# An input tile without padding, a mean transformed once, and a second tile for a rounded angle, in an adaLN kernel with an S4D convolution and a token mixer

## The chip, the cores and the metric

The kernel runs on one core of one Trainium2 chip. The metric is the device time of one execution in microseconds (us), and lower is better. One core has TensorE (PE, matmuls; its weight loads are listed as PEld), VectorE (DVE), ScalarE (ACT), GpSimd (POOL) and SyncE (SP), which issues most of the DMA transfers. Each engine works through its own instructions in order; engines wait for each other by semaphores. SBUF is the on-chip memory of 128 partitions, PSUM the memory that matmuls write.

## What is computed

The input `A_u` has 2048 tokens of 448 channels. The reference, cut to what matters:

```python
mod = (silu(c) @ w_mod)                     # six vectors: sa, ca, ga, sb, cb, gb
h = layernorm(x) * (1 + ca) + sa
x = x + ga * A_ref(h)                       # S4D: a long convolution per channel
h = layernorm(x) * (1 + cb) + sb
x = x + gb * B_ref(h)                       # mixer: an MLP over the tokens

def A_ref(u):
    A = -exp(log_A_real) + 1j * A_imag;  C = (C_real + 1j * C_imag) * dt
    P = exp((A * dt)[:, :, None] * arange(L))        # 448 x 256 x 2048
    K = 2 * einsum("dn,dnl->dl", C, P).real
    y = irfft(rfft(u^T, 2L) * rfft(K, 2L))[:L]
    return y^T + u * D_skip
```

## The kernel before

**The convolution kernel K.** The 448 channels are cut into 28 groups of 16, each in two halves of the 256 states, so 56 steps `s`, and these into seven windows of eight. Per channel and state a complex exponential is needed. Its exponents and phases come from matmuls against a table (`tab`) with rows `lex` and `lph`; ScalarE turns them into magnitudes (`mag`) and sines and cosines (`xe`, `xg`, `gs`); GpSimd multiplies the `G` factors (lines 716 and 717) and `m` (line 696), VectorE the `E` factors (lines 718 to 722); TensorE contracts them in `st_kgen` (line 743). At the start of a window `window(s)` makes the magnitudes of its eight steps.

**Parameters.** The rows in `lex` and `lph` are prepared for 128 channels at a time, q = 0 to 3. `chain(q)` is a generator whose small steps on VectorE are taken a few at a time, by `more(n)`, between other work. Its `split` writes a value as a high and a low part (`hl`, two buffers) on GpSimd and stores both to DRAM (`pars`, line 406), from where the groups load them. `phase()` leaves the parts of a phase in `ph` and `p64`, with `u` as a scratch tile; `angles()` follows and rounds an angle. For q of 2 and 3 `angles()` comes right after `phase()`, for q = 1 they stand apart.

**The transform of the input.** `x_load` puts the input rows into `xt`, [128, 16, 450]: a partition holds 16 successive tokens of 448 channels, each row followed by two spare columns. Twenty DMAs do this, each for 32 partitions and two or four rows; twelve are issued by SyncE, eight by GpSimd. `u_stats` (lines 543, 544) makes mean and variance of each token on VectorE. At step 8 `u_scale` makes the inverse deviations `rs` and writes the negative mean of each token into the first spare column, and `u_table` scales the transform's table `wu` by `rs`. `u_rows` then runs 32 times: a matmul of a scaled table with one row of `xt` and its mean column, 449 columns, and on VectorE an eviction (line 574) that adds the mean's column to the others and multiplies by `mod[1]`. Two evictions fill a tile `yt` (three buffers), which SyncE stores to `yu_d`. `u_cols` (lines 606, 610) is the second half of the transform, from step 17 on, evicted as `uo`. Later `xt` also receives parts of `w_mod`.

**Order.** PE, ACT, DVE and POOL run in the order in which the program issues their instructions. SyncE's DMAs run in written order up to step 8; from there to the last part of the convolution a planner orders them. The lists `act` and `dve` hold evictions that `flush` issues later on that engine. In the window at step 8 the first pass of the loop (`e == 0`) ends with seven warm-up matmuls, `warm(7)`, on TensorE; from the second pass on each has rows of `u_rows`. PSUM tiles of the transforms share three buffers (`pms`, tag `ms`).

After the 56 steps come the products in frequency, the inverse transform, the second layernorm, and the mixer (lines 1377 to 1379 and 1540 to 1542), which takes the second half of the time.

Of the kernel before, what the change touches and what calls it, by code (L numbers as in the profile page):

```python
# [11 lines left out]
F32 = mybir.dt.float32  # L12
# [3 lines left out]
ALU = mybir.AluOpType  # L16
# [5 lines left out]
L, D, N, F = 2048, 448, 256, 1792  # L22
P = 128
# [10 lines left out]
MAGIC = 1.5 * 2.0**23  # L34
# [198 lines left out]
def tile_adaln_s4d_mixer(ctx, tc, i, out):  # L233
    nc = tc.nc
    x = i["A_u"][0]
# [9 lines left out]
    mod = [None] * 3 + [cp.tile([P, D], F32, name=f"mod{k}") for k in range(3, 6)]  # L245
# [7 lines left out]
    with ExitStack() as es:  # L253
        V, S, G, T = nc.vector, nc.scalar, nc.gpsimd, nc.tensor
        tt, ts, stt = V.tensor_tensor, V.tensor_scalar, V.scalar_tensor_tensor
# [11 lines left out]
        pms = es.enter_context(tc.tile_pool(name="pms", bufs=3, space=PSUM))  # L267
# [8 lines left out]
        xp = spec.enter_context(tc.tile_pool(name="xp", bufs=1))  # L276
# [25 lines left out]
        nc.sync.dma_start(ldt[:, 1:3], ldt_v[P : 3 * P].rearrange("(q p) -> p q", p=P))  # L302
        for k in range(2):
            nc.sync.dma_start(ldt[64 * k : 64 * k + 64, 3:4], ldt_v[3 * P : D].rearrange("(q p) -> p q", q=1))
        xt = xp.tile([P, 16, D + 2], F32, name="xt")

        def x_load(r0, n, eng=nc.sync):
            for g in range(4):
                to = xt[32 * g : 32 * g + 32, r0 : r0 + n, 0:D]
                (nc.sync if r0 > 7 and g < 2 else eng).dma_start(to, x.rearrange("(s n h r) d -> h s n r d", s=2, h=2, r=16)[g // 2, g % 2, :, r0 : r0 + n])  # L310


        mg = cg.tile([P, 2, P], BF16, name="mg")
# [18 lines left out]
        wu = xp.tile([P, P], F32, name="wu")  # L332
# [12 lines left out]
        for q in range(4):  # L345
            r = slice(32 * q, 32 * q + 1)
# [32 lines left out]
        dve, act, aside = [], [], []  # L379
# [7 lines left out]
        def chain(q):  # L387


            n = min(P, D - P * q)  # L390
            f = N * n // P
            cr, ci, a, aim = (raws[q][nm][:, 0:f] for nm in ("A_C_real", "A_C_imag", "A_log_A_real", "A_A_imag"))
            xa, ya, s, t, u, ph, p64 = (
                qp.tile([P, N], F32, tag=nm, name=nm)[:, 0:f] for nm in ("xa", "ya", "s", "t", "u", "ph", "p64")
            )

            def split(src, places):
                hl = qp.tile([P, 2, N], F32R, tag="hl", name="hl", bufs=2)[:, :, 0:f]
                eng = G if aside or q == 1 else V
                eng.tensor_copy(hl[:, 0], src)  # L400
                yield
                eng.tensor_tensor(hl[:, 1], src, hl[:, 0].bitcast(F32), ALU.subtract)
                for k, v in places:
                    for m in range(P // n):
                        to = pars[q][v, k, 0:n, :, m * f : (m + 1) * f]
                        nc.sync.dma_start(to, hl[n * m : n * m + n].bitcast(F32))
                yield


            def phase():  # L410
                ts(ph, aim, dt4[:, q : q + 1], None, ALU.mult)
                yield
                ts(u, ph, MAGIC, MAGIC, ALU.add, ALU.subtract)
                yield
                tt(ph, ph, u, ALU.subtract)
                yield
                yield from split(ph, [(0, 0)])

                ts(u, ph, MAGIC7, MAGIC7, ALU.add, ALU.subtract)
                yield  # L420
                tt(p64, ph, u, ALU.subtract)
                yield
                yield from split(p64, [(1, 0)])

            def angles():
                ts(xa, xa, 4 * i2p, -0.5, ALU.mult, ALU.add)
                yield
                ts(cr, cr, 0.0, 0.5, ALU.is_ge, ALU.subtract)
                yield
                tt(xa, xa, cr, ALU.mult)  # L430
                yield
                ts(ci, ci, 0.0, 0.5, ALU.is_ge, ALU.subtract)
                yield
                stt(xa, xa, 0.5, ci, ALU.add, ALU.mult)
                yield
                stt(xa, ph, 63.0, xa, ALU.mult, ALU.add)
                yield
                ts(p64, xa, MAGIC, MAGIC, ALU.add, ALU.subtract)
                yield
                tt(xa, xa, p64, ALU.subtract)  # L440
                yield
                yield from split(xa, [(2, 0)])

            for to, src in (xa, cr), (ya, ci):
                if q > 1:
                    S.activation(to, src, AF.Abs, scale=0.5)
                else:
                    ts(to, src, -0.5, None, ALU.mult)
                    yield
                    stt(to, src, 0.5, to, ALU.mult, ALU.max)  # L450
                    yield
            tt(s, xa, ya, ALU.add)
            yield
            tt(ya, ya, xa, ALU.subtract)
            yield
            ts(s, s, 2.0**-120, None, ALU.max)
            yield
            V.reciprocal(xa, s)
            yield
            tt(ya, ya, xa, ALU.mult)  # L460
            yield

            ts(t, s, 2.0**-40, 2.0**80, ALU.is_lt, ALU.mult)
            yield
            stt(s, t, 1.0, s, ALU.max, ALU.mult)
            yield
            if q == 1:
                while not late_steps:
                    yield "logs"
                yield from phase()  # L470
            tmp[q] = a, s, u, xa, ya
            while q in tmp:
                yield "logs"
            if q == 1:
                yield from angles()
            ya = u
            yield from split(a, [(0, 1), (1, 1)])
            stt(s, t, -80 * math.log(2.0) / 2.0**80, s, ALU.mult, ALU.add)
            yield
            stt(s, ya, 0.5, s, ALU.mult, ALU.add)  # L480
            yield
            ts(s, s, ldt2[:, q : q + 1], None, ALU.add)
            yield
            yield from split(s, [(2, 1)])
            yield "exponents"

            if q > 1:
                yield from phase()

            if q > 1:  # L490
                yield from angles()
# [45 lines left out]
        mv = xp.tile([P, 16, 2], F32, name="mv")  # L537
        rs = xp.tile([P, 16], F32, name="rs")
        nm = xp.tile([P, 16], F32, name="nm")

        def u_stats(r):
            st = xp.tile([P, 6], F32, tag="st", name="st", bufs=2)
            V.bn_stats(st, xt[:, r, 0:D])
            V.bn_aggr(mv[:, r], st)

        def u_scale():

            tt(nm, rs, rs, ALU.mult)
            stt(nm, mv[:, :, 1], EPS, nm, ALU.add, ALU.mult)
            ts(nm, nm, -0.5, 1.5, ALU.mult, ALU.add)  # L550
            tt(rs, rs, nm, ALU.mult)
            ts(xt[:, :, D : D + 1], mv[:, :, 0:1], -1.0, None, ALU.mult)

        yts, wurs = {}, {}

# [5 lines left out]
        def u_rows(n):  # L561

            R, g = divmod(n, 4)
            gp, gl = divmod(g, 2)
            if gl == 0:
                yts[R, gp] = xp.tile([P, 2, D], F32, tag="yt", name="yt", bufs=3)
            if g == 0 and R < 6:
                u_table(R + 2)
            pm = pms.tile([P, D + 1], F32, tag="ms", name="pu")
            p = slice(64 * gl, 64 * gl + 64)  # L570
            T.matmul(pm, wurs[R][p, gp], xt[p, 2 * R + gp, 0 : D + 1], start=True, stop=True)

            def out():
                stt(yts[R, gp][:, gl], pm[:, 0:D], pm[:, D : D + 1], mod[1], ALU.add, ALU.mult)
                if gl:
                    nc.sync.dma_start(
                        yu_d[:, :, :, R, 2 * gp : 2 * gp + 2].rearrange("o k c g d -> (o k c) (g d)"),
                        yts.pop((R, gp)).rearrange("p g d -> p (g d)"),
                    )

            dve.append(out)
# [71 lines left out]
        def warm(n):  # L653

            g = made_k[0] // 2
            free = (kgs[g - 1] if g - 1 in kgs else kg_tile(g))[:, 4:8]
            for _ in range(n):
                T.matmul(free, ones[:, 0:P], ones[:, 0:256], start=made_k[0] % 2 == 0, stop=made_k[0] % 2 == 0, skip_group_check=True)
# [136 lines left out]
        pl, pu, pz, pv, pk = {}, {}, {}, {}, {}  # L795
# [232 lines left out]
        rows, cols, pieces = iter(range(32)), iter(range(16)), [0, 0]  # L1028
# [42 lines left out]
        def window(s):  # L1071
# [12 lines left out]
            for e in range(BATCH):  # L1084
# [30 lines left out]

                if s == 8 and e == 0:
                    warm(7)
                if s in (8, 16):
                    some(u_rows, rows, ((0, 2, 2, 2, 2, 0, 2, 2) if s == 8 else (2, 2, 2, 2, 2, 0, 1, 1))[e])
                elif s == 24 and e in (0, 2, 4, 6, 7):  # L1120
                    some(u_cols, cols, 1)
# [452 lines left out]
```

## Time and profile before

| | us |
|---|---|
| three runs | 669.04, 670.04, 670.37 |
| median | 670.04 |
| profiled execution | 668.55 |
| its span in the trace | 666.7 |
| PE busy | 615.8 (92%) |
| DVE busy | 442.9 (66%) |
| ACT busy | 440.4 (66%) |
| POOL busy | 269.7 (40%) |

The profile comes from one execution of its own. Times in its views are microseconds from the start of the span. A busy share is a mean over stages with different limits; POOL is idle in the second half. In a row of the timeline stand start, duration, engine, line, operation, output<-inputs and count, and in brackets the idle time before it and what ended that; rows of the same line next to each other are merged. "issue" stands for a wait that the profile cannot put down to anything. In a row of groups stand total busy time and mean nanoseconds of one.

### The profile page before, as it was taken

What the parts mean: (1) busy time and instruction counts of PE and PEld (TensorE: products, weight loads), DVE (VectorE), ACT (ScalarE), POOL (GpSimd) and SP (SyncE); (2) the same over time, 40 slices, a digit from 0 to 9 for tenths busy, and PEclk for the clock granted to TensorE, in tenths of its full rate; (3) what the DMA queues carried; (4) which work ended last, traced back from release to release, by engine and by line L of the source; (5) the groups of instructions that cost most, each with busy time, mean ns of one, the idle gap of its engine ahead of it and who ended that gap; (6) DMA issues with size and microseconds to landing.
All of it is one profiled execution on the core that took longest, in us unless ns stands there. A gap on an engine that the chain in (4) does not pass through costs nothing.

```text
span 666.7 us, 19151 instructions
## 1 busy us (share of the span) xinstructions
PE 615.8 (92%) x7637; PEld 445.0 (67%) x7637; DVE 442.9 (66%) x850; ACT 440.4 (66%) x828; POOL 269.7 (40%) x349
## 2 busy tenths in 40 slices
PE   1868899999899999999989899999999999999997
PEld 0545455445346565656645577788999999999997
DVE  8989789689696686869655678787522553333331
ACT  6978698899689999999678678886222532222220
POOL 7885588488589878797463000000000000000000
PEclk9998899999899899999999899999999999999999
DMA  6696747598775458567787999946664265555530
GB/s 157 191 215 174 253 157 247 197 257 260 221 236 175 107 128 215 168 185 222 210 281 238 262 243 249 220 125 200 169 189 137 71 188 161 165 162 167 163 116 28
DMA packets 99601, 125.14 MB, mean 188 GB/s; under 512 B 13780, under 2 KB 81144, under 8 KB 99512
## 3 DMA queue, kind: packets, MB, share of 16 engines
q1 hardware_dynamic: 98568, 121.30, 63.9%
q0 software_dynamic: 944, 2.62, 1.6%
q8 instruction: 60, 0.98, 0.6%
q14 instruction: 29, 0.24, 0.1%
HBM read 88.53 MB, written 34.87 MB: 185 GB/s over the span
## 4 chain that ended last, share of the span: by engine, by line
PE 60%; DMA 13%; ACT 9%; POOL 6%; DVE 5%; issue 4%; SPq 2%; ACTq 0%; DVEq 0%; POOLq 0%
PE o L1541 7%; PE o L1540 7%; PE o L1542 7%; PE acc L1377 6%; PE acc L1378 6%; PE acc L1379 6%; PE xe L646 5%; PE kg L743 5%; DMA v_d<-vt 4%; DMA w<-in_B_w_dram 3%; PE xg L646 3%; DMA lph<-pars 2%; PE pu L606 2%; PE vv L874 2%; POOL G L716 2%
## 5 line engine op out<-in xcount | busy, mean ns | idle before, releaser
L218 ACT CAST whi<-w 128x896 fp32r<-128x896 f32 x64 | 59.7, 939 | 138.2 <-PE o L1541 81.3
L227 DVE TENSOR_TENSOR wlo<-w,whi 128x896 fp32r<-128x896 f32 x64 | 68.1, 1086 | 41.2 <-ACT whi L218 38.1
L716 POOL TENSOR_TENSOR G<-mag,gs 128x512 f32<-128x512 f32 x56 | 71.9, 1284 | 42.2 <-ACT gs L712 42.2
L1377 PE MATMUL acc<-h3h,whi 128*128 128x448 f32 x224 | 83.0, 370 | 2.4 <-ACT h3h L1444 0.9
L1378 PE MATMUL acc<-h3l,whi 128*128 128x448 f32 x224 | 81.6, 364 | 0.6 <-DVE h3l L1451 0.4
L1541 PE MATMUL o<-ul,whi 128*128 128x448 f32 x224 | 81.3, 363 | 0.0
L1540 PE MATMUL o<-uh,whi 128*128 128x448 f32 x224 | 81.2, 362 | 0.0
L1379 PE MATMUL acc<-h3h,wlo 128*128 128x448 f32 x224 | 80.7, 360 | 0.0
L1542 PE MATMUL o<-uh,wlo 128*128 128x448 f32 x224 | 80.6, 360 | 0.0
L743 PEld LDWEIGHTS kg<-E,G 128*32 128x32 f32 x3584 | 54.7, 112 | 30.2 <-issue 19.0
L717 POOL TENSOR_TENSOR G<-mag,gs 128x512 f32<-128x512 f32 x56 | 71.9, 1284 | 0.0
L646 PE MATMUL xg<-tab,lph 64*128 64x512 f32 x112 | 63.4, 566 | 8.2 <-DVE E L722 5.3
L743 PE MATMUL kg<-E,G 128*32 128x64 f32 x3584 | 63.9, 224 | 4.8 <-issue 3.4
L646 PE MATMUL xe<-tab,lph 64*128 64x512 f32 x112 | 63.5, 567 | 0.3 <-issue 0.2
L1545 DVE TENSOR_TENSOR y<-o,x 128x448 f32<-128x448 f32 x16 | 10.0, 627 | 78.9 <-PE o L1542 78.9
L696 POOL TENSOR_TENSOR m<-mag,w 128x512 f32<-128x512 f32 x53 | 55.8, 1053 | 4.1
L1377 PEld LDWEIGHTS acc<-h3h,whi 128*128 128x128 f32 x224 | 42.0, 188 | 16.1 <-ACT h L1449 2.8
L708 ACT ACTIVATE ab<-xe 128x512 f32<-128x512 f32 x56 | 33.8, 604 | 19.5 <-PE xg L646 10.2
L1378 PEld LDWEIGHTS acc<-h3l,whi 128*128 128x128 f32 x224 | 42.1, 188 | 3.6 <-DVE h3l L1451 1.0
L1540 PEld LDWEIGHTS o<-uh,whi 128*128 128x128 f32 x224 | 42.0, 188 | 3.4
L1542 PEld LDWEIGHTS o<-uh,wlo 128*128 128x128 f32 x224 | 41.9, 187 | 3.0
L1379 PEld LDWEIGHTS acc<-h3h,wlo 128*128 128x128 f32 x224 | 41.9, 187 | 2.9
(249 smaller groups left out, 1406.6 us busy)
## 6 DMA issues: line engine op xcount, KB each, us to landing
w<-in_B_w_dram SPq DMA_DIRECT2D x64, 224.0 KB
w<-in_B_w_dram SPq DMA_DIRECT2D x32, 448.0 KB
yu_d<-yt SPq DMA_DIRECT2D x16, 448.0 KB
yi<-yu_d SPq DMA_DIRECT2D x32, 224.0 KB
us_d<-uo SPq DMA_DIRECT2D x16, 448.0 KB
u<-us_d SPq DMA_DIRECT2D x64, 112.0 KB
v_d<-vt SPq DMA_DIRECT2D x32, 224.0 KB
vt<-v_d SPq DMA_DIRECT2D x14, 448.0 KB
```

Source lines behind the costliest of these rows:

```text
L218: self.nc.scalar.copy(hi, w)
L227: eng.tensor_tensor(lo, w, hi.bitcast(F32), ALU.subtract)
L646: T.matmul(out[k], lhs[r], rhs[r], start=start, stop=stop)
L716: G.tensor_tensor(Gt[:, 1], mg_, v32(sg), ALU.mult)
L717: G.tensor_tensor(Gt[:, 0], mg_, v32(cg_), ALU.mult)
L743: T.matmul(kg[32 * q : 32 * q + 32, m], Gt[:, c, d], E[:, c, d], start=h == 0 and c == 0 and m == 0, stop=h == 1 and c == 1, skip_group_ch ...
L1377: nc.tensor.matmul(acc[f], hi[:, fs], h3h[:, r], start=r == 0, stop=False)
L1378: nc.tensor.matmul(acc[f], hi[:, fs], h3l[:, r], start=False, stop=False)
L1379: nc.tensor.matmul(acc[f], lo[:, fs], h3h[:, r], start=False, stop=r == 15)
L1540: nc.tensor.matmul(o, hi[:, ks], uh[kh][:, k], start=kh == 0 and k == 0, stop=False)
L1541: nc.tensor.matmul(o, hi[:, ks], ul[kh][:, k], start=False, stop=False)
L1542: nc.tensor.matmul(o, lo[:, ks], uh[kh][:, k], start=False, stop=kh == 1 and k == 6)
```

## The change

Three edits. The input tile loses its two spare columns, so that each load is one contiguous piece per partition. The mean's part of the row transform is made once for all rows: `u_scale` writes minus mean times `rs` into a small tile `means` (one half of the columns for each half of the partitions, zero elsewhere), `u_means` transforms it with one matmul by the unscaled table and copies it back, and the evictions of `u_rows` take their scalar from there. For q of 2 and 3 `angles()` rounds into `u` in place of `p64`.

```diff
-        xt = xp.tile([P, 16, D + 2], F32, name="xt")
+        xt = xp.tile([P, 16, D], F32, name="xt")
 ...
-                to = xt[32 * g : 32 * g + 32, r0 : r0 + n, 0:D]
-                (nc.sync if r0 > 7 and g < 2 else eng).dma_start(to, x.rearrange("(s n h r) d -> h s n r d", s=2, h=2, r=16)[g // 2, g % 2, :, r0 : r0 + n])
+                to = xt[32 * g : 32 * g + 32, r0 : r0 + n].rearrange("p r d -> p (r d)")
+                rows = x.rearrange("(s n h r) d -> h s n (r d)", s=2, h=2, r=16)[g // 2, g % 2]
+                (nc.sync if r0 > 7 and g < 2 else eng).dma_start(to, rows[:, r0 * D : (r0 + n) * D])
 ...
-                ts(p64, xa, MAGIC, MAGIC, ALU.add, ALU.subtract)
+                whole = u if q > 1 else p64
+                ts(whole, xa, MAGIC, MAGIC, ALU.add, ALU.subtract)
                 yield
-                tt(xa, xa, p64, ALU.subtract)
+                tt(xa, xa, whole, ALU.subtract)
 ...
+        means = xp.tile([P, 2, 16], F32, name="means")
+        G.memset(means, 0.0)
 ...
-            ts(xt[:, :, D : D + 1], mv[:, :, 0:1], -1.0, None, ALU.mult)
+            for h in range(2):
+                p = slice(64 * h, 64 * h + 64)
+                stt(means[p, h], mv[p, :, 0], -1.0, rs[p], ALU.mult, ALU.mult)
+
+        def u_means():
+            pm = pms.tile([P, 2, 16], F32, tag="ms", name="pn")
+            T.matmul(pm, wu, means, start=True, stop=True)
+            act.append(lambda: S.copy(means, pm))
 ...
-            pm = pms.tile([P, D + 1], F32, tag="ms", name="pu")
+            pm = pms.tile([P, D], F32, tag="ms", name="pu")
-            T.matmul(pm, wurs[R][p, gp], xt[p, 2 * R + gp, 0 : D + 1], start=True, stop=True)
+            T.matmul(pm, wurs[R][p, gp], xt[p, 2 * R + gp], start=True, stop=True)
 ...
-                stt(yts[R, gp][:, gl], pm[:, 0:D], pm[:, D : D + 1], mod[1], ALU.add, ALU.mult)
+                mean = means[:, gl, 2 * R + gp : 2 * R + gp + 1]
+                stt(yts[R, gp][:, gl], pm, mean, mod[1], ALU.add, ALU.mult)
 ...
                 if s == 8 and e == 0:
                     warm(7)
+                    u_means()
```

More of the change, by code (lines that the diff above doesn't have):

```diff
@@ L539, in tile_adaln_s4d_mixer @@
         nm = xp.tile([P, 16], F32, name="nm")
+        means = xp.tile([P, 2, 16], F32, name="means")
+        G.memset(means, 0.0)
         def u_stats(r):
             st = xp.tile([P, 6], F32, tag="st", name="st", bufs=2)
-            V.bn_stats(st, xt[:, r, 0:D])
+            V.bn_stats(st, xt[:, r])
             V.bn_aggr(mv[:, r], st)
```

## The prediction

> **What bounds the kernel now.** I read the page's chain first, then the waits of the stretches in which the edited lines run, then the timeline of each engine there.
>
> ```profile
> PE 60%; DMA 13%; ACT 9%; POOL 6%; DVE 5%; issue 4%; SPq 2%; ACTq 0%; DVEq 0%; POOLq 0%
> ```
>
> TensorE carries 60% of the chain that ended last, but most of that is the mixer at the end, which the change does not touch. Everything edited runs before 182 us, where the chain changes hands every few microseconds. So I price each edit in its own place.
>
> Rounded angle (lines 438 and 440). The waits of VectorE between 150 and 200 us, the timelines there (start, duration, engine, line), and the windows:
>
> ```profile
> DVE p L438 <- POOL hl L402: 2.7, 1, 2.7
> ```
> ```profile
> 176.74 0.23 DVE L438 TENSOR_SCALAR p<-xa 128x128 f32<-128x128 f32 x1 [2.68 <-POOL hl L402]
> ...
> 177.21 1.27 DVE L610 SCALAR_TENSOR_TENSOR uo<-mod,svt,pu 128x448 f32<-128x448 f32 x2
> ```
> ```profile
> 177.94 1.01 PE L606 MATMUL pu<-yi,s 64*64 64x448 f32 x3 [2.23 <-DVE uo L610]
> ```
> ```profile
> 180.48 1.98 PE L781 MATMUL y<-wc,ks 64*64 64x64 f32 x62 [0.78 <-DVE uo L610]
> ```
> ```profile
> 184.39 0.60 ACT L708 ACTIVATE ab<-xe 128x512 f32<-128x512 f32 x1 [5.05 <-PE xg L646]
> ```
> ```profile
> 178.94 0.29 POOL L400 CAST hl<-xa 128x128 fp32r<-128x128 f32 x1 [2.23 <-DMA pars<-hl]
> 179.31 0.46 POOL L402 TENSOR_TENSOR hl<-xa,hl 128x128 fp32r<-128x128 f32 x1
> 179.72 1.28 POOL L716 TENSOR_TENSOR G<-mag,gs 128x512 f32<-128x512 f32 x1
> ...
> 182.51 1.05 POOL L696 TENSOR_TENSOR m<-mag,w 128x512 f32<-128x512 f32 x1
> 186.56 1.29 POOL L716 TENSOR_TENSOR G<-mag,gs 128x512 f32<-128x512 f32 x1 [3.00 <-ACT gs L712]
> ```
> ```profile
> 194.00:198.00 4.00, 4.00 (x88) 2.01 (x82) 4.00 (x7) 3.71 (x8) 3.92 (x6) 1.00 0.44 156
> ```
>
> The reader is to see one chain of cause. VectorE may not overwrite `p64` until GpSimd has read it, and stands still 2.68 us. The eviction `uo` behind it comes late, TensorE waits 2.23 us for a free bank, then again before `y`, ScalarE waits 5.05 us for the next phases, and GpSimd 3.00 us for `gs`. From 186.56 us on GpSimd is full (3.92 of 4.00 us in the last row; columns are PE, weight loads, DVE, ACT, POOL, clock, DMA share, GB/s), and the last G products of the chain follow without a gap.
>
> **The change part by part.** The sum is made against the profiled execution, 668.55 us (span 666.7); the median of the three runs is 670.04, 1.49 more.
>
> *Part C, the free tile.* For q=2 and 3 the rounded angle goes to `u`, whose last reader is line 421, on VectorE itself, so only order on one engine is left. For q=2 the views name no wait at line 438, so it is worth nothing. For q=3 the instruction at 176.74 starts 2.68 earlier, at 174.06, and `uo` at 174.53 instead of 177.21. Its input was ready: GpSimd's reading was all that VectorE waited for. TensorE's three matmuls move from 177.94 to about 175.3, the second `uo` pair and `y` follow 2.7 us earlier or more, and ScalarE can begin the phase of step 25 near 180. What is late next is GpSimd: its `hl<-xa` at 178.94 waits for a store of `pars`, which the edit does not move, so its products of step 24 stay at 179.72 and `m` ends at 182.51+1.05=183.56. Then the product at 186.56 can start: 3.00 us earlier. ScalarE's `gs` buffers come free only when the first product ends (179.72+1.28=181.00), and three activations of 0.6 us from there are done near 182.6, in time. GpSimd is full behind it, so the 3.00 us go on. Ends: 0 (something else holds step 25) and -3.8 (also the 0.82 us that `y` takes longer at 180.48 than at 76.86, further down). I take -3.0, the GpSimd row.
>
> *Part B, the mean.* Rows of the stage (VectorE, TensorE, SyncE, GpSimd, a window) and groups of the whole run:
>
> ```profile
> 64.40 0.37 DVE L549 SCALAR_TENSOR_TENSOR nm<-mv,nm 128x16 f32<-128x16 f32 x1
> ...
> 65.01 0.58 DVE L551 TENSOR_TENSOR rs<-rs,nm 128x16 f32<-128x16 f32 x1
> 65.52 0.17 DVE L552 TENSOR_SCALAR xt<-mv 128x16 f32<-128x16 f32 x1
> ...
> 67.90 1.28 DVE L574 SCALAR_TENSOR_TENSOR yt<-pu,mod 128x448 f32<-128x448 f32 x2
> ...
> 76.12 1.28 DVE L574 SCALAR_TENSOR_TENSOR yt<-pu,mod 128x448 f32<-128x448 f32 x2 [3.08 <-DMA yu_d<-yt]
> ```
> ```profile
> 62.78 0.94 PE L658 MATMUL kg<-ones 128*128 128x256 bf16 x7
> 64.81 0.50 PE L646 MATMUL xe<-tab,lex 64*128 64x512 f32 x1 [1.10 <-ACT mag L675]
> ...
> 76.86 1.16 PE L781 MATMUL y<-wc,ks 64*64 64x64 f32 x62 [2.26 <-DVE yt L574]
> ```
> ```profile
> 70.94 0.98 SPq L576 DMA_DIRECT2D yu_d<-yt  x2
> ```
> ```profile
> 11.95 0.52 POOL L916 CAST wm<-ph 128x256 fp32r<-128x256 f32 x1 [2.81 <-DVE ph L975]
> ```
> ```profile
> 78.00:82.00 4.00, 4.00 (x20) 2.93 (x18) 3.93 (x8) 2.24 (x5) 0.00 (x0) 0.57 0.94 283
> ```
> ```profile
> L743 PE MATMUL kg<-E,G 128*32 128x64 f32 x3584 | 63.9, 224 | 4.8 <-issue 3.4 <-POOL G L717 0.8 <-DVE E L722 0.6
> ```
> ```profile
> L571 PE MATMUL pu<-xt,wur 64*128 64x449 f32 x64 | 24.1, 621 | 0.7 <-ACT yk L787 0.7
> L574 DVE SCALAR_TENSOR_TENSOR yt<-pu,mod 128x448 f32<-128x448 f32 x32 | 20.4, 680 | 7.9 <-PE pu L571 4.8 <-DMA yu_d<-yt 3.1
> L610 DVE SCALAR_TENSOR_TENSOR uo<-mod,svt,pu 128x448 f32<-128x448 f32 x32 | 20.2, 673 | 2.5 <-PE pu L606 2.5
> ```
>
> Removed: one of 449 columns in 64 matmul passes (0.22% of 24.1 us, 0.05 us) and the 0.17 us of line 552. The `yt` evictions take their scalar from SBUF as line 610 does (673 against 680 ns): 32 x 7 ns = 0.2 us, put at nothing because the chain there runs over stores and GpSimd. Added: a memset on GpSimd before its first casts, 0.17 us by line 552, which the 2.81 us idle at 11.95 hides (0.17 if not); two small operations on VectorE, each 0.17 (line 552) to 0.58 (line 551), taken as line 549's 0.37; one matmul of 32 columns in two passes, 0.2 to 1.2 us by lines 743 and 571, taken as 0.4, nearest to line 743; one copy of 32 columns on ScalarE, under the 0.60 us of a 512-column row, which TensorE's own delay hides (0.6 if not).
>
> The new wait is the serious piece. `u_means` stands on TensorE right behind the seven warm-up matmuls, which end at 63.72, and needs VectorE's second operation: 65.52+2x0.37=66.26. Queued behind it is the exponent matmul of 64.81; it now starts at 66.26+0.4=66.66, 1.9 us late (1.0 to 3.1 by the ends), and with it all of TensorE until it stops at 76.86-2.26=74.6. ScalarE's exponentials and the first `yt` wait for that. Cover: SyncE did not store the first `yt` before 70.94 although it was done at 67.90+1.28=69.18, so 1.76 us of the delay are free and 0.1 to 0.2 remain on the store, whose landing releases 76.12 and so 76.86. If that cover is gone, the whole 1.9 is paid.
>
> The clock: TensorE's 2.26 us gap before 76.86 was followed by a granted clock of 0.57 over 4 us, which costs 0.43x4=1.7 us against full speed. The new gap, 63.72 to 66.26, is 2.5 us, so I expect a slow stretch there too; but the delayed work then fills the later gap, and the later slow stretch goes. The two cancel within a few tenths. The Trainium skill, "TensorE: Matmul & The Clock Gate", section "Part 1: The HAM clock gate", lets the clock fall only after an idle window of about 3.4 us. By that rule the new gap costs no clock and the sum would be 0.1 us better; the row after the 2.26 us gap disagrees with it, and I go by the row. Part B: +0.2, ends -1.7 (the late slow stretch goes, no new one comes) and +3.6 (1.9 and a slow stretch of 1.7, neither covered nor given back).
>
> *Part A, the loads.* All 20 issues remain; each carries 32 pieces of 3584 or 7168 bytes instead of 64 or 128 of 1792. SyncE's issues of `xt` (least, median, most), then the queues between 34 and 50 us (packets, MB, share of 16 engines), then who stood still:
>
> ```profile
> L310 SPq DMA_DIRECT2D xt<-in_A_u_dram x12: 312/428/584, 27.3 to 37.6; - x12
> ```
> ```profile
> q1 hardware_dynamic: 1637, 2.59, 78.4%
> q0 software_dynamic: 253, 0.90, 24.3%
> ```
> ```profile
> 44.35 0.63 DVE L543 BATCH_NORM_STATS2 st<-xt 128x6 f32<-128x448 f32 x1 [1.45 <-DMA xt<-in_A_u_dram]
> ```
> ```profile
> 52.28 0.69 DVE L718 TENSOR_TENSOR E<-m,xe 128x512 f32<-128x512 f32 x1 [0.29 <-issue]
> ```
> ```profile
> 48.06 0.43 PE L743 MATMUL kg<-E,G 128*32 128x64 f32 x6 [3.36 <-issue]
> ```
>
> An issue may fall from 428 to 312 ns on SyncE, 12 x 0.12 = 1.4 us at most, hidden under the transfers themselves, which keep the engines full (78.4+24.3%); GpSimd's eight issues are taken to keep their time. GpSimd's queue already moved `xt` in packets of 0.90 MB/253 = 3.6 KB at 0.90 MB/(0.243 x 16 x 16 us) = 14.5 GB/s per engine, SyncE's queue its 1.6 KB packets at 12.9. So longer pieces buy some 13%, about 1 us over the 9 us before 44. That shortens VectorE's 1.45 us wait, but next stands TensorE's stall of 3.36 us, which ends at 48.06 whatever VectorE does: of the gain only about the 0.29 us at 52.28 can pass. Ends: 0, and -1.7 (1.45+0.29, if the stall goes as well; VectorE has no more idle time there). I take -0.3. The Trainium skill, "DMA: Bandwidth & Descriptors", section "Specifications", puts line rate at pieces of 512 bytes and more. By that rule the 1792-byte pieces lose nothing already, this part is 0, and the sum is 0.3 us worse.
>
> Sum: -0.3+0.2-3.0 = -3.1, so 665.45 for a run like the profiled one and 666.95, say 667.0, beside the median.
>
> **The rivals.** *The new wait is paid in full.* A slow stretch after the 2.5 us gap delays the first `yt` well past SyncE's 70.94, and the late one stays: part B is +3.6, the time 667.0+3.4=670.4, no change to speak of. For it: the clock row. Against: 1.76 us of cover, and work that fills the later gap.
>
> *The fetch stall grows: slower.* Nothing that the profile shows ended TensorE's 3.36 us stall at 48.06, in the stretch where the DMA engines were full; I take it for instructions arriving late. If pieces four times as long hold an engine longer per turn, it grows. Doubled, it costs 3.36 and another slow stretch of 1.7: 667.0+5.1=672.1. With that stretch it decides once the stall is 3.1+1.3-1.7=2.7 us longer, near 6 us. Against: the last `xt` lands near 44.3, as the stall begins.
>
> *The stall shrinks.* The faster loads also free the engines for it: part A is -1.7 in place of -0.3, the time 665.6. For it: same place, full engines.
>
> *The free tile frees nothing.* VectorE no longer waits at 174, but a later store or load holds step 25 or the window after it, all the more since SyncE's order there is a planner's and may come out anew: part C is 0, the time 670.0. Against: the GpSimd rows.
>
> **How the numbers follow.** Forecast 0.52 (own range 665.6 to 668.4), stall shrinks 0.14, wait paid 0.16, nothing freed 0.06, stall grows 0.12. The range 664.4 to 670.6 holds all but the last and the tails. Three runs lay between 669.04 and 670.37, so 0.2% (1.3 us) is about what can be told: faster 0.66, same 0.22, slower 0.12.
>
> **What would show it.** Right: no wait at the rounding line near 174 us, TensorE's `pu` there without its 2.23 us, GpSimd's product after `m` without 3.00 us idle; a TensorE wait of about 2.5 us for VectorE's `means` near 64 us, the first `yu_d` store within 0.3 us of its old place relative to the `pars` stores; VectorE's wait for `xt` under 1 us. Wrong: a clock near 0.5 between 67 and 73 us with the one at 78 still there, or an instruction stall near 45 us that is far from 3.4 us.

## The result and the profile after

| | median us | runs | ratio to before on the same chip, 95% interval |
|---|---|---|---|
| changed kernel, first time | 664.12 (662.86 to 666.05) | 4 | 0.9927 [0.9899, 0.9954] |
| a second time | 666.63 | 12 | 0.9963 [0.9929, 0.9997] |
| a third time | 667.56 | 12 | 0.9980 [0.9952, 1.0008] |

The change makes the kernel faster, but by less than the first four runs say. Weighted by their intervals the three ratios give 0.9955: 3.0 us of 670.04, or 667.0. That mean is rougher than it looks: the first and the third ratio differ by 0.0053, more than their two intervals together allow for (0.0039). A ratio is not the quotient of the two medians, and leaves out a slow run where there was one, as in the second line; the quotients of the medians in this document differ from the ratios by up to 0.2% (in the first line 664.12, against 670.2 for the runs beside it, would be 0.9909). The first median, 664.12, lies 0.3 us under the range that was forecast. The profile below is of one of those four runs: 663.95 us, span 662.2, against 668.55 and 666.7 before.

The shares of the chain that ended last, and the rounded angle: the waits' row is gone, and the timelines of VectorE, TensorE, ScalarE and GpSimd (start, duration, engine, line) with one window (PE, weight loads, DVE, ACT, POOL, clock, DMA share, GB/s) read:

```profile
PE 61%; DMA 9%; ACT 9%; DVE 9%; issue 5%; POOL 4%; SPq 2%; DVEq 0%; ACTq 0%; POOLq 0%
```
```profile
172.14 0.23 DVE L440 TENSOR_SCALAR u<-xa 128x128 f32<-128x128 f32 x1
172.40 0.29 DVE L442 TENSOR_TENSOR xa<-xa,u 128x128 f32<-128x128 f32 x1
172.61 1.27 DVE L623 SCALAR_TENSOR_TENSOR uo<-mod,svt,pu 128x448 f32<-128x448 f32 x2
```
```profile
172.79 1.52 PE L619 MATMUL pu<-yi,s 64*64 64x448 f32 x8
...
175.09 1.16 PE L794 MATMUL y<-wc,ks 64*64 64x64 f32 x62 [0.77 <-DVE uo L623]
```
```profile
172.90 0.60 ACT L721 ACTIVATE ab<-xe 128x512 f32<-128x512 f32 x1 [0.78 <-PE xg L659]
...
177.46 0.60 ACT L721 ACTIVATE ab<-xe 128x512 f32<-128x512 f32 x1
```
```profile
177.85 0.29 POOL L401 CAST hl<-xa 128x128 fp32r<-128x128 f32 x1 [3.11 <-DMA pars<-hl]
178.22 0.45 POOL L403 TENSOR_TENSOR hl<-xa,hl 128x128 fp32r<-128x128 f32 x1
178.63 1.28 POOL L729 TENSOR_TENSOR G<-mag,gs 128x512 f32<-128x512 f32 x1
...
181.43 1.05 POOL L709 TENSOR_TENSOR m<-mag,w 128x512 f32<-128x512 f32 x1
182.44 1.28 POOL L729 TENSOR_TENSOR G<-mag,gs 128x512 f32<-128x512 f32 x1
```
```profile
178.00:182.00 4.00, 3.66 (x24) 1.82 (x20) 4.00 (x8) 3.06 (x7) 3.84 (x6) 1.00 0.58 175
```

VectorE rounds without a wait, `pu` runs through, ScalarE's 5.05 us are gone, and no product of GpSimd waits for `gs`. Two things are to be seen besides. `y` takes 1.16 us where it took 1.98, and the granted clock from 178 to 182 us is 1.00 (before it was 0.50, shown with the runs). And GpSimd's cast of `xa` now stands alone in waiting for a store of `pars`, 3.11 us.

The mean (TensorE, VectorE, SyncE, windows):

```profile
62.26 0.94 PE L671 MATMUL kg<-ones 128*128 128x256 bf16 x7
65.68 0.41 PE L563 MATMUL pn<-means,wu 128*128 128x32 f32 x2 [2.49 <-DVE means L558]
...
76.81 1.16 PE L794 MATMUL y<-wc,ks 64*64 64x64 f32 x62 [0.38 <-DVE yt L587]
```
```profile
64.94 0.69 DVE L558 SCALAR_TENSOR_TENSOR means<-mv,rs 64x16 f32<-64x16 f32 x2
...
69.67 1.28 DVE L587 SCALAR_TENSOR_TENSOR yt<-pu,means,mod 128x448 f32<-128x448 f32 x2 [2.23 <-PE pu L583]
```
```profile
70.97 1.79 SPq L589 DMA_DIRECT2D yu_d<-yt  x2
```
```profile
66.00:70.00 4.00, 4.00 (x74) 2.66 (x74) 1.73 (x4) 1.77 (x5) 2.13 (x5) 0.65 0.28 79
...
78.00:82.00 4.00, 3.37 (x18) 1.80 (x18) 3.93 (x8) 3.66 (x7) 0.00 (x0) 1.00 0.95 241
```

The new wait is 2.49 us long, SyncE's first store of `yu_d` stands at 70.97 as it stood at 70.94, and the slow stretch has moved from 78 to 66 us.

The loads (queues between 34 and 50 us, VectorE, TensorE):

```profile
q1 hardware_dynamic: 1280, 2.62, 77.5%
q0 software_dynamic: 192, 0.92, 24.8%
```
```profile
44.68 0.63 DVE L547 BATCH_NORM_STATS2 st<-xt 128x6 f32<-128x448 f32 x1 [1.56 <-DMA xt<-in_A_u_dram]
```
```profile
48.62 0.31 PE L756 MATMUL kg<-E,G 128*32 128x64 f32 x6 [3.70 <-issue]
```

SyncE's queue moved 1.2% more bytes in 22% fewer packets, in the same share of the engines' time. VectorE waits for `xt` as long as before, and TensorE's stall is there.

### The profile page after: what moved, and what is told of

It is laid out like the page before. It is cut to its first block, busy times and chain, and to the rows that moved or that the text cites. A ratio compares the mean times of both kernels' runs of the same rounds, so it can differ in the third digit from the quotient of the medians.

```text
span 662.2 us, 19159 instructions
## 1 busy us (share of the span) xinstructions
PE 612.0 (92%) x7639; PEld 442.3 (67%) x7639; DVE 443.0 (67%) x851; ACT 440.2 (66%) x829; POOL 268.8 (41%) x350
## 3 DMA queue, kind: packets, MB, share of 16 engines
q0 software_dynamic: 816, 2.62, 1.6%
## 4 chain that ended last, share of the span: by engine, by line
PE 61%; DMA 9%; ACT 9%; DVE 9%; issue 5%; POOL 4%; SPq 2%; DVEq 0%; ACTq 0%; POOLq 0%
PE o L1555 7%; PE o L1554 7%; PE o L1556 7%; PE acc L1391 6%; PE acc L1392 6%; PE acc L1393 6%; PE xe L659 6%; PE kg L756 5%; DMA w<-in_B_w_dram 3%; PE xg L659 2%; PE pu L583 2%; PE vv L887 2%; DMA v_d<-vt 2%; ACT mag L688 2%; POOL G L729 2%
## 5 line engine op out<-in xcount | busy, mean ns | idle before, releaser
L659 PE MATMUL xg<-tab,lph 64*128 64x512 f32 x112 | 62.0, 554 | 6.8 <-DVE E L735 5.2
L659 PE MATMUL xe<-tab,lph 64*128 64x512 f32 x112 | 61.9, 553 | 0.3 <-issue 0.2
L1555 PEld LDWEIGHTS o<-ul,whi 128*128 128x128 f32 x224 | 42.0, 188 | 2.3
```

What stands on the lines that cost most here:

```text
L659: T.matmul(out[k], lhs[r], rhs[r], start=start, stop=stop)
L1555: nc.tensor.matmul(o, hi[:, ks], ul[kh][:, k], start=False, stop=False)
```

## The experiments

**How the profiles are compared.** One kernel's times spread by 8 us or more on one chip, so beside the ratios I use a ladder: the start of ScalarE's first activation of `ab` in each of the 56 steps, minus that in the profile before. For equal code it is not equal. The changed kernel's three profiles stand at step 8 at -1.4, -1.0 and +1.8 us, at step 24 at -2.0, -1.2 and +4.2. But between two near steps it is steadier: from step 24 to step 32 they gain 2.1, 3.0 and 3.3. So I read part C from that difference, and don't read parts A and B from a single profile.

**One part at a time.** The first kernel is before with part C alone:

```diff
-                ts(p64, xa, MAGIC, MAGIC, ALU.add, ALU.subtract)
+                whole = u if q > 1 else p64
+                ts(whole, xa, MAGIC, MAGIC, ALU.add, ALU.subtract)
...
-                tt(xa, xa, p64, ALU.subtract)
+                tt(xa, xa, whole, ALU.subtract)
```

> The kernel before with part C alone (the angle of q=2 and 3 rounded into u). Theory 1, read from the ladder of steps in the two profiles: VectorE's wait and step 25's 5.05 us are gone, but GpSimd can start its stretch only about 1.1 us earlier because its cast of xa still waits for a store of pars; C is worth 2.1 to 2.4 us, the ratio to before 0.9965. Theory 2, the prediction: GpSimd's 3.00 us pass on whole, ratio 0.9955. Theory 3: C is nearly the whole of the 6.1 us between the medians and A and B are nothing, ratio 0.991. In the trace the product after m near 182 us has no idle time under all three.

Measured 0.9969 [0.9949, 0.9988], -2.1 us; the ladder gains 2.96 from step 24 to 32. The interval holds theory 1 and the prediction alike.

The second is before with `means` and `u_means` alone; `xt` keeps its spare columns and its loads (the eviction; the rest of part B is as in the change):

```diff
-            stt(yts[R, gp][:, gl], pm[:, 0:D], pm[:, D : D + 1], mod[1], ALU.add, ALU.mult)
+            stt(yts[R, gp][:, gl], pm, mean, mod[1], ALU.add, ALU.mult)
```

> The kernel before with part B alone (means and u_means; xt keeps its two spare columns and its loads, p64 stays). Theory 1: the new wait of 2.5 us near 64 us is covered by SyncE's first yu_d store and the late slow stretch near 78 us goes; step 8 starts 0.5 us earlier, the whole is -0.5 to -1 us, ratio 0.999. Theory 2, the prediction's own number: +0.2 us, ratio 1.000. Theory 3, the wait is paid in full: +3.6 us, ratio 1.005, with a slow clock at 67 to 70 and again at 78 to 82.

Measured 0.9979 [0.9957, 1.0000], -1.4 us. The wait is not paid in full (1.005). In its profile the new wait was 2.06 us, and no slow stretch followed it, nor one at 78 us.

The third is the changed kernel with `p64` again:

```diff
-                whole = u if q > 1 else p64
-                ts(whole, xa, MAGIC, MAGIC, ALU.add, ALU.subtract)
+                ts(p64, xa, MAGIC, MAGIC, ALU.add, ALU.subtract)
...
-                tt(xa, xa, whole, ALU.subtract)
+                tt(xa, xa, p64, ALU.subtract)
```

> The changed kernel without part C (rounding into p64 again): A and B. Theory 1, the ladder of the two profiles at step 24: -1.7 to -2.0 us, ratio 0.9973, with VectorE's wait of about 2.7 us at the rounding line and TensorE's 2.2 us back. Theory 2, the prediction: -0.1 us, ratio 1.000. Theory 3: A and B carry more than C, -3.5 us or more, ratio below 0.995. The difference of this run to B alone is the loads' share: 0 if the longer pieces bring nothing, -1 us if they do.

Measured 1.0010 [0.9981, 1.0038]. My theory 1 fell: the -1.95 us by step 24 in the first pair of profiles were not the edits'. The stall at the rounding is back, and ScalarE's wait behind it is longer than before's 5.05 us:

```profile
185.00 0.60 ACT L720 ACTIVATE ab<-xe 128x512 f32<-128x512 f32 x1 [6.28 <-PE xg L658]
```

The fourth is the changed kernel with the padded tile and the row loads (the tile; the loads are again as before):

```diff
-        xt = xp.tile([P, 16, D], F32, name="xt")
+        xt = xp.tile([P, 16, D + 2], F32, name="xt")
```

> The changed kernel without part A (xt with its two spare columns again, loads of one row per piece): B and C. Theory 1: the pieces bring nothing, and this is the changed kernel's time, ratio 0.9925 to 0.994. Theory 2: the loads shift the clock or the instruction stall near 45 us by 0.5 to 1 us; ratio 0.9945. In the trace theory 2 has step 7 start 0.9 us later than in the changed kernel, theory 1 within 0.3 us of it.

Measured 0.9963 [0.9935, 0.9992]. Step 7 began 0.6 us earlier than in the first profile of the changed kernel, so neither theory's row holds, and the ratio is that of the changed kernel's second run. The loads bring nothing that can be seen.

**The changed kernel again.**

> The changed kernel again, beside the kernel before and the three runs that follow, as many times as them. Theory 1: its earlier 6.1 us were partly luck of which stretches the clock was halved in (27.2 us of them in the profile before, 17.0 in the one after, and one kernel's times spread over 8 us); with more runs it comes to about -3 us, ratio 0.9955, as B and C together gave -2.5 us. Theory 2: the loads (A) make up the difference to B and C together, and it stays near -5 us, ratio 0.9927.

Theory 1: 0.9963. Without A it was the same 0.9963, on another chip.

**The new wait taken away.** `u_means` stands one pass later, just ahead of the rows, its copy on VectorE:

```diff
-            act.append(lambda: S.copy(means, pm))
+            dve.append(lambda: V.tensor_copy(means, pm))
...
                     warm(7)
+                if s == 8 and e == 1:
                     u_means()
```

> The changed kernel with u_means in the second pass of the loop of step 8, just ahead of the first rows, and its copy on VectorE: the wait of 2.49 us is no longer ahead of the exponents. Theory 1, the prediction's cover: SyncE's first yu_d store near 71 us does not move by more than 0.3 us, and the time is the changed kernel's within 0.5 us. Theory 2: what the wait costs is the halved clock behind it, 3.4 or 6.8 us long near 66 us; it goes, and the time is 1.0 to 1.7 us better than the changed kernel's.

Measured 0.9966 [0.9941, 0.9991], by the ratio the same as the changed kernel beside it (0.9963). By the medians it is 2.6 us slower (669.28 against 666.63), so that the time is equal within 0.5 us, as theory 1 said, is not shown; theory 2's gain is not seen by either. SyncE's first `yu_d` store stands at 70.36, 0.6 us earlier. TensorE and two windows:

```profile
66.55 0.41 PE L563 MATMUL pn<-means,wu 128*128 128x32 f32 x2
...
76.16 1.89 PE L794 MATMUL y<-wc,ks 64*64 64x64 f32 x62 [1.53 <-DVE yt L587]
```
```profile
66.00:70.00 4.00, 4.00 (x63) 2.17 (x56) 3.84 (x8) 3.01 (x7) 2.03 (x5) 1.00 0.46 149
76.00:80.00 4.00, 3.84 (x70) 3.40 (x70) 3.90 (x8) 1.92 (x4) 0.58 (x2) 0.57 0.95 256
```

The wait and the slow stretch near 66 are gone, and the later wait before `y` and a slow stretch at 76 are back. One idle gap of TensorE is exchanged for another, and the new wait's cover, as the prediction named it, is this later gap.

**GpSimd's wait taken away.** The last split of q=3 goes to the tile of `A_C_real`, free by then, in place of a third use of `hl`:

```diff
-            def split(src, places):
-                hl = qp.tile([P, 2, N], F32R, tag="hl", name="hl", bufs=2)[:, :, 0:f]
+            def split(src, places, spare=None):
+                hl = spare or qp.tile([P, 2, N], F32R, tag="hl", name="hl", bufs=2)[:, :, 0:f]
...
-                yield from split(xa, [(2, 0)])
+                yield from split(xa, [(2, 0)], raws[q]["A_C_real"].rearrange("p (k f) -> p k f", k=2).bitcast(F32R) if q > 2 else None)
```

> The changed kernel with the last split of q=3 written to the tile of A_C_real, which is free by then, so that GpSimd's cast of xa no longer waits for a store of pars (3.11 us at 177.85). Theory 1, GpSimd's start is what now limits the stretch: the casts move to 174.7, the first product of step 24 to about 176.9 (held by the second activation of gs), 1.7 us earlier, and the time is 1.5 us better than the changed kernel's. Theory 2, ScalarE and TensorE limit step 25 as well: the product of step 25 starts no earlier than 181.5, the gain is under 0.9 us. Theory 3: nothing is gained.

Measured 0.9948 [0.9912, 0.9984]. GpSimd:

```profile
176.06 0.29 POOL L401 CAST A_C_real<-xa 128x128 fp32r<-128x128 f32 x1
176.43 0.46 POOL L403 TENSOR_TENSOR A_C_real<-xa,A_C_real 128x128 fp32r<-128x128 f32 x1
177.78 1.29 POOL L729 TENSOR_TENSOR G<-mag,gs 128x512 f32<-128x512 f32 x1 [0.89 <-ACT gs L725]
...
181.59 1.28 POOL L729 TENSOR_TENSOR G<-mag,gs 128x512 f32<-128x512 f32 x1
```

The cast follows the one before without a wait, and the product waits for ScalarE instead. That stage ran 1.3 us later here than in the first profile of the changed kernel, and the product of step 25 still starts 0.85 us earlier. Against the start of step 24 that is 2.2 us, as in theory 1; the time does not separate the theories.

Both edits together:

> The last two edits together on the changed kernel. If both first theories hold for their edits (cover; GpSimd's start), 1.5 us better than the changed kernel; if the halved clock behind the wait counts too, 2.5 to 3.2 us better; if neither moves the end, the changed kernel's time.

Measured 0.9928 [0.9901, 0.9955], 666.78 us (six runs). Ratio and median disagree here: by the first it is 2.3 us better than the changed kernel, by the second 0.15 us worse (666.63), so the time decides nothing. Its profile lost 5.5 us by step 5 and gained 4.54 from step 24 to 32.

**The wait and the clock told apart.** Before, with spare matmuls in the gap ahead of the stalled `pu`:

```diff
             for j in range(2):
                 for b in range(2):
+                    if fill and j == 0 and b == 1:
+                        warm(fill.pop())
...
                 elif s == 24 and e in (0, 2, 4, 6, 7):
+                    if e == 7:
+                        fill.append(16)
```

> The kernel before with 16 spare matmuls of 256 columns (about 0.13 us each, 2.0 us) put on TensorE into the gap of 2.23 us ahead of its stalled pu near 176 us; VectorE's wait at the rounding line stays. It splits part C into the wait itself and the halved clock behind it, which stood at 177 to 184 us in all three profiles with the wait and in none of the four without. Theory 1, the clock carries as much as the wait: the halved stretch at 177 goes, y falls from 1.98 to 1.16 us and the phases behind it by 0.7, step 25 starts on ScalarE 1.5 to 2.1 us earlier against step 24 and GpSimd's idle 3.00 us falls to 1.0 to 1.5; the time is 1.5 us better than before. Theory 2, the wait carries it: GpSimd's idle time stays above 2.3 us, under 0.7 us gained. Theory 3: the spare matmuls do not keep the clock; nothing changes.

TensorE, VectorE, GpSimd and a window of this kernel, then the same window before and in the second and third kernels, which have the wait too:

```profile
174.44 1.92 PE L660 MATMUL kg<-ones 128*128 128x256 bf16 x16
176.62 0.98 PE L608 MATMUL pu<-yi,s 64*64 64x448 f32 x6 [0.25 <-DVE uo L612]
...
178.37 1.16 PE L783 MATMUL y<-wc,ks 64*64 64x64 f32 x62 [0.77 <-DVE uo L612]
```
```profile
175.42 0.23 DVE L438 TENSOR_SCALAR p<-xa 128x128 f32<-128x128 f32 x1 [2.56 <-POOL hl L402]
```
```profile
179.24 1.28 POOL L718 TENSOR_TENSOR G<-mag,gs 128x512 f32<-128x512 f32 x1
...
182.03 1.05 POOL L698 TENSOR_TENSOR m<-mag,w 128x512 f32<-128x512 f32 x1
183.04 1.28 POOL L718 TENSOR_TENSOR G<-mag,gs 128x512 f32<-128x512 f32 x1
```
```profile
178.00:182.00 4.00, 3.63 (x83) 2.20 (x84) 3.34 (x7) 1.42 (x4) 3.42 (x5) 1.00 0.87 258
```
```profile
178.00:182.00 4.00, 3.23 (x64) 2.04 (x67) 1.75 (x3) 1.34 (x3) 2.98 (x4) 0.50 0.80 223
```
```profile
178.00:182.00 4.00, 4.00 (x45) 1.68 (x38) 3.20 (x6) 1.12 (x3) 3.60 (x4) 0.50 0.96 293
```
```profile
178.00:182.00 4.00, 2.87 (x48) 1.68 (x52) 2.17 (x4) 0.72 (x2) 2.99 (x4) 0.54 0.65 173
```

VectorE waits as before (2.56 us), yet with the gap filled the clock stays at 1.00, `y` takes 1.16 us, and GpSimd's 3.00 us of idle time are gone altogether, more than theory 1 said. From the first product of step 24 to that of step 25 GpSimd takes 183.04-179.24 = 3.80 us, as in the changed kernel (182.44-178.63 = 3.81); before it took 186.56-179.72 = 6.84. The ladder gains only 1.50 us from step 24 to 32. Up to step 31 GpSimd's products stand 2.34 us earlier against step 24; the rest is lost just before step 32, probably to a slow stretch that began at 213.9 us here and at 218.1, just ahead of step 32, in the profile before. The time, 0.9999 [0.9968, 1.0029], does not show it: the interval holds the 1.5 us as well as nothing, and this profile took 2 us longer than before's behind the last step.

**The spare tile on before, and the last comparison.**

> The kernel before with part C and the spare tile for the last split, without A and B. Theory 1, A and B bring next to nothing and the gain lies around 175 to 200 us: from step 24 to step 32 it gains 3.8 to 4.5 us as the two earlier runs with the spare tile, and the ratio to before is 0.993 to 0.995, that of the changed kernel with the spare tile. Theory 2, B brings 1 us or more of its own: ratio above 0.996.

> The changed kernel with the spare tile again, beside the changed kernel on the same chip. Theory 1, from the ladder (steps 24 to 32 gained 1.3 us more with it than in the mean of the five profiles with part C alone): 1.3 us better than the changed kernel, ratio to before 0.9945. Theory 2: the later stages take it back; the same as the changed kernel.

> The changed kernel a third time, the other half of that comparison. The two earlier ratios were 0.9927 (4 runs) and 0.9963 (12 runs). If the sum of the prediction holds, 0.9955, -3.0 us; if the first draw was the typical one, 0.993.

Part C and the spare tile on before: 0.9951 [0.9920, 0.9983]. The changed kernel with the spare tile: 664.49 us, 0.9946 [0.9919, 0.9973]; without it, on that chip: 667.56 us, 0.9980. The gain on the ladder from step 24 to 32:

| kernels | gain, us | mean |
|---|---|---|
| with the wait: before, B alone, A and B | 0, -0.08, -1.02 | -0.4 |
| the same, gap filled | 1.50 | 1.5 |
| part C in it, six profiles | 2.12, 2.96, 2.35, 3.01, 2.03, 3.31 | 2.6 |
| part C and the spare tile, four profiles | 3.81, 4.54, 4.52, 3.78 | 4.2 |

The groups do not overlap. The spare tile gives a further 1.5 us there, and its four ratios (0.9928 to 0.9951) lie below two of the changed kernel's three. By the ratios no kernel with it is separated from the changed kernel; the medians on one chip lie 0.8 us apart in one pair (665.82, 666.63) and 3.1 in another (664.49, 667.56).

## Why the prediction was right, and where it was not

**The whole.** 667.0 was forecast, and the three comparisons come to 667.0. That it is so near is partly luck: the three lie up to 3.6 us apart, and the parts were not all of the size that was forecast. What no part of the forecast held is that the time at half clock differs from run to run. By the trace's record (without the stretch at the very end) it was 27.3 us in the profile before, of 668.55 us, and 17.1, 17.1 and 27.3 in the three of the changed kernel, which took 663.95, 664.17 and 670.00. The first median, 664.12, is probably low for that reason.

**Part C, -3.0.** Right in size on the ladder: 2.6+0.4 = 3.0 us between the kernels with and without the wait; by the times C alone is -2.1. The chain of cause is right up to ScalarE. The step that failed is that GpSimd's 3.00 us were the price of VectorE's 2.68 alone. In the one profile with the gap filled, VectorE still waited 2.56 us and GpSimd no longer idled ahead of step 25's product, so the 3.00 us were the price of the half clock behind TensorE's gap, which the wait brings about. To step 32 that profile shows 1.50 us, or 1.5+0.4 = 1.9 of the 3.0; what the wait costs without the half clock therefore lies somewhere between nothing and 1.1 us. The prediction had the row (`y` 1.98 in place of 1.16) and left it for the end of the range. What is late next was named rightly as GpSimd behind the store of `pars`, and the run with the spare tile puts a price on it: 1.5 us.

**Part B, +0.2.** The wait was 2.49 us where 2.54 was worked out, the first store moved by 0.03 us, and in the changed kernel the slow stretch came behind the new gap and the later one went, all as written. In the profile of B alone neither came, so the exchange of the one for the other is not the rule. B alone measured -1.4 us with an interval that ends at 0, A and B 1.0010; the size of B stays open. Taking the wait away brought no gain.

**Part A, -0.3.** Not shown. The step that failed is that longer pieces move faster: SyncE's queue went from 2.59 MB in 78.4% of the engines' time to 2.62 MB in 77.5%, 2% more per busy time and not 13%. "VectorE's wait for xt under 1 us" did not come true in the first profile (1.56); over all of them it is 0.66 to 3.73 where it shows with A (six of eight) and 0.41 to 1.45 without. The page of the Trainium skill that the prediction weighed, "DMA: Bandwidth & Descriptors", section "Specifications", would have it at 0, and the trace agrees. What the prediction left out is a possible loss. VectorE waits early on for `A_C_real` in the second profile of the changed kernel, where before it had it in time:

```profile
19.24 0.29 DVE L450 TENSOR_SCALAR xa<-A_C_real 128x256 f32<-128x256 f32 x1 [1.48 <-DMA A_C_real<-in_A_C_real_dram]
```
```profile
18.76 0.28 DVE L448 TENSOR_SCALAR xa<-A_C_real 128x256 f32<-128x256 f32 x1
```

Such a wait stands in five of eight profiles with A and in one of six without. Step 5 began 0.2 to 5.5 us later than before's in the eight (median 1.0), and -0.02 to +0.4 in the six. How the longer pieces would bring the wait about is not shown: until 26 us only GpSimd issues loads of `xt`, and SyncE issues `A_C_real` (at 16.53 us before, at 16.98 here), so the two share the DMA engines but not a queue. The times do not confirm a loss: A and B against B alone is 0.3% slower, the spare tile with A and B against without 0.05% faster, both inside their intervals. Whether A costs anything in the end stays open.

**The rivals.** TensorE's stall, which the profiles put down to nothing, did not grow: its longest piece was 2.8 to 3.8 us in ten of the fourteen profiles, with A and without, and 1.1 to 2.7 in four others with A (two of these have a second piece of 1.45 and 0.97). That it is instructions arriving late, no run shows. Where it was shortest, 1.12 us in the third profile of the changed kernel, VectorE waited 3.73 us for `xt` instead, and nothing was gained. The wait was not paid in full, and the free tile did free something.

## What to carry to other kernels

An idle gap of TensorE can cost twice, once as the wait and once as the half clock behind it; here the second was the greater part, all of GpSimd's 3.00 us in the one profile that tells them apart. Filling the gap with spare matmuls got that back in its stage with the wait still there, though the whole time (0.9999) does not show it. A gap may just move when it is removed in one place, so look for the next one before counting a gain. And before a difference of 1% is read from one pair of profiles, profile the same code again: here equal code differed by 6 us at step 24, and only the difference between two near steps was steady.

## What the runs showed of the hardware

The clock is granted in pieces: by its record every slow stretch but the one at the very end lasted 3.4 or 6.8 us, at places that shift from one execution to the next. Gaps of 1.84 to 3.27 us ahead of `pu` brought one of 6.8 us in all three kernels that had them (B alone, before, A and B); a gap of 0.25 us brought none. A gap does not always bring one: in B alone none followed the 2.06 us ahead of `pn` at 62.6 us, nor the 3.22 us of the stall at 44.8. The Trainium skill, "TensorE: Matmul & The Clock Gate", section "Part 1: The HAM clock gate", tells of a free-running window of 3413 ns, and the lengths agree; that a whole window must be idle does not agree with gaps this short.

A GpSimd operation can hold up one of VectorE. The same operation, on VectorE before (GpSimd idle from 29.31 to 30.17 us) and in the second kernel with A, B, C and the spare tile, with what GpSimd did then:

```profile
29.50 0.42 DVE L465 SCALAR_TENSOR_TENSOR s<-t,s 128x256 f32<-128x256 f32 x1
```
```profile
31.20 1.36 DVE L467 SCALAR_TENSOR_TENSOR s<-t,s 128x256 f32<-128x256 f32 x1
```
```profile
28.05 1.26 POOL L717 TENSOR_TENSOR G<-mag,gs 128x512 f32<-128x512 f32 x1
30.17 1.27 POOL L716 TENSOR_TENSOR G<-mag,gs 128x512 f32<-128x512 f32 x1 [0.86 <-ACT gs L712]
```
```profile
30.98 1.30 POOL L730 TENSOR_TENSOR G<-mag,gs 128x512 f32<-128x512 f32 x1
```

It took 0.42 us alone and 1.36 beside GpSimd's product, ending 0.28 us after it. In three more profiles it began under that product; it took 1.37 or 1.38 us and ended 0.28 or 0.29 after it. The Trainium skill, "SBUF — State Buffer", section "SBUF: two separate sides", calls the pair of ports that the two share an exclusive lock, and the rows agree. What the hold-up costs further on is not shown: in this profile step 2 began 3.4 us late, but in two of the other three, both without A, it began 0.07 us earlier and 0.38 later than before's.
